# Gate product of the turned weight pieces two slots later, in a fused linear attention and two-MoE kernel on one Trainium2 core

## The chip, the cores and the metric

The kernel runs on 1 core of one Trainium2 chip. The metric is the device time of one execution in microseconds (us), the median of the runs shown.

## The reference

Three layers follow one another, all in float32. Layer 1 is linear attention over 2 batches, 8 heads, 576 positions and head dimension 64, with 128 random features. Its output is laid out as 1152 tokens of width 512. Layer 2 is a dense feed-forward layer over all tokens. Layer 3 sends each token to the one of 8 experts with the largest gate logit, with a capacity of 288 tokens per expert; positions are counted in token order.

```python
q_p, k_p = phi(q * scale), phi(k * scale)          # exp of projections less their maximum
attn = (q_p @ (k_p.T @ v)) / (q_p @ k_p.sum() + 1e-6)
x = attn as [1152, 512]
h = x @ w_in; g = h * (1 / (1 + exp(-1.702 * h)))   # [1152, 2048]
x = g @ w_out                                      # [1152, 512]
logits = x @ w_gate; expert = argmax(logits)       # 8 experts
# each expert takes its first 288 tokens: relu(x @ w1[e]) @ w2[e], scaled by the softmax weight
```

## The kernel before, in words

**Precision.** A float32 matrix product is done as three products on TensorE, of a rounded high part and the remainder (`mm3`, L81 to L84: high by high, high by low, low by high). So every weight and every activation is split into `hi` and `lo`. A split takes a cast on ScalarE and a subtraction on VectorE or GpSimd.

**Tokens and slots.** The 1152 tokens are four groups G of 288. The second layer is cut into 16 slices m of 128 hidden features. A slot n of the list `seq` (L570 to L574) makes one slice of one group: `do_h` (12 matmuls into one of two PSUM banks, then gelu on ScalarE). Two slots later `do_consume` uses the gelu. Groups 0, 1 and 3 are mixed in slots 0 to 47 (the 16 slots of group 2 follow as 48 to 63). From slot 7 to slot 39 the pattern is G = 0, 1, 3, repeated.

For groups 0 and 2 the gelu is split: ScalarE writes `ghi` (L596) and the full value g32 (L598; the trace calls it g), VectorE writes `glo` (L599), and `do_y` multiplies both into the output. For groups 1 and 3 only the routing logits are wanted at first. ScalarE writes one full value g1 (L591), which waits in a list until four of them are there (two of each group). Then `run_lg` (L635 to L641) multiplies them with `wp`, the product of w_out and w_gate for that slice. By the order of the list `run_lg` runs in slots 10, 14, 20, 26, 32, 38, 43, 47 and 49, after the `do_h` of that slot. The values g1 and g32 share the buffers of one tag, `g1`, with five of them; a slot's gelu gets whichever buffer is free.

**Decoding weights.** The weights arrive as 8-byte numbers in 512 KB pieces (two pieces for each slice, one of w_in, one of w_out). `decode` turns a piece into float32 by three VectorE operations (L220, L223, L226), a cast on ScalarE (L232) and a subtraction on GpSimd (L233). Six pieces are decoded during the attention, the other 26 beside the slots by `decode_slot(n)` (L901), one for each slot from slot 9 on (slot 25 has the last). `paced` puts each VectorE step behind the newest `glo` in VectorE's order.

**The gate product.** For `wp` a decoded w_out piece is turned in 32x32 blocks on VectorE (`do_wt`, L481, tile `wt`, one buffer for two slices). For every second slice `do_wg` (L483) multiplies `wt` on TensorE (32 small matmuls, L488), ScalarE copies the result, and one slot later `do_wp` (L494) makes `wp` from it. `do_wg` runs `P["wgl"]` = 2 slots after the decode of the odd slice. The pieces of slices 9, 11, 13 and 15 are decoded in slots 13, 17, 21 and 25, so their gate products stand in slots 15, 19, 23 and 27, at the end of the slot.

**Third layer.** The experts' first products (`do_h2`, 16 slots) use the same tags `ghi` and `glo` for their relu (`hhi`, L832, `hlo`, L833) and the same two PSUM banks. Expert weights are split by ScalarE (L818) and VectorE (L819) beside them.

**Order.** The order in each engine's queue comes from a scheduler that works through the instructions by priority, that is by the order of the program, and takes a buffer for a tile when one is free. Each engine then works its queue in order.

Of the kernel before, what the change touches and what calls it, by code (L numbers as in the profile page):

```python
# [8 lines left out]
F32 = mybir.dt.float32  # L9
F32R = mybir.dt.float32r  # L10
BF16 = mybir.dt.bfloat16
I32 = mybir.dt.int32
ACTF = mybir.ActivationFunctionType
ALU = mybir.AluOpType
AX = mybir.AxisListType.X
P = dict(ahead=2, kvlag=2, t2=3, n=5, x=6, dec=(13, 16, 19, 22, 25, 28), tailstep=0.5, zero=26, w0=12, loadlag=10, pv=(0, 4), l1=3, l3=5, wgl=2, hpt=30, dmin=0.9, dc=1, dd=2, dlead=6, dpace=1)


@with_exitstack
def linear_attention__moe__top1_moe_kernel(  # L20
# [18 lines left out]
    E = moe2_w1.shape[0]  # L39
# [5 lines left out]
    GS = 288  # L45
# [12 lines left out]
    const = ctx.enter_context(tc.tile_pool(name="const", bufs=1, side="left"))  # L58
    xp = ctx.enter_context(tc.tile_pool(name="xp", bufs=1, side="left"))
    gp = ctx.enter_context(tc.tile_pool(name="gp", bufs=3, side="left"))  # L60
# [5 lines left out]
    attB = stB.enter_context(tc.tile_pool(name="attB", bufs=1, side="left", reuse_waits="tile"))  # L66
    stA = ExitStack()
    attA = stA.enter_context(tc.tile_pool(name="attA", bufs=1, side="right", reuse_waits="tile"))
    def bank(tag, name):
        return psA.tile([128, 512], F32, tag=tag, name=name, bufs={"A": 2, "B": 3, "C": 1, "M": 1, "L": 1}[tag])  # L70
# [20 lines left out]
    def load_rows(src, kind, b, p, parts=1):  # L91
        t = attA.tile([128, NU, D], F32, tag="raw", name="qk_raw", bufs=6)
        heads = src[b, 4 * p:4 * p + 4]
        per = 4 // parts
        for i in range(parts):
            hs_ = slice(i * per, (i + 1) * per)
            nc.sync.dma_start(
                out=t[:, JF * per * i:JF * per * (i + 1)].rearrange("p (h j) d -> p h (j d)", j=JF),
                in_=heads[hs_, 0:SF].rearrange("h (p j) d -> p h (j d)", j=JF),
            )  # L100
        for h in range(2):
            nc.sync.dma_start(
                out=t[64 * h:64 * h + 64, 16:18],
                in_=heads.rearrange("(u h) s d -> h s u d", h=2)[h, SF:S],
            )
        raws[kind, b, p] = t
# [93 lines left out]
    def w_in(m):  # L200
        hi, lo = W["in", m // 4]
        c = slice((m % 4) * 128, (m % 4) * 128 + 128)
        return hi[:, :, c], lo[:, :, c]
# [50 lines left out]
    def at(s, f):  # L254
        pend.setdefault(s, []).append(f)
# [70 lines left out]
    def do_kv_out(b, p):  # L326
        t = attB.tile([128, 4, VW], F32, tag="kvs", name="kvs", bufs=4)
        nc.scalar.copy(t.rearrange("p h n -> p (h n)"), kvp.pop((b, p))[:, :4 * VW])
        kvs[b, p] = t
# [71 lines left out]

    npre = len(P["dec"])
    wseq = [(kd, m) for m in range(NF) for kd in ("in", "out")]
# [19 lines left out]
    for kd, b, p in pairs:  # L423
        ps_ = pos[kd, b, p]
        for x in (kd, "v") if kd == "k" else (kd,):
            if (x, b, p) not in raws:
                at(max(0, ps_[0] - P["loadlag"]), lambda x=x, b=b, p=p: load_rows(srcs[x], x, b, p))
        if kd == "k":
            if b > 0:
                at(pos["k", 0, p][4] + P["kvlag"] + 1, lambda b=b, p=p: place_v(b, p))  # L430
            else:
                at(P["pv"][p], lambda p=p: place_v(0, p, mark["M", P["pv"][p]]))
            for d in range(5):
                at(ps_[d] + P["kvlag"], lambda s=ps_[d]: do_KV(s))
            at(ps_[4] + P["kvlag"], lambda b=b, p=p: do_kv_out(b, p))
        else:
# [16 lines left out]
    NB = DM // 32  # L453
# [22 lines left out]
    wts, wus = {}, {}  # L476

    def do_wt(m):
        if m % 2 == 0:
            wts[m // 2] = gp.tile([128, NB, 2, 32], F32, tag="wt", name="wt", bufs=1)  # L480
        nc.vector.transpose(wts[m // 2][:, :, m % 2], wfs.pop(m).rearrange("p (b j) -> p b j", j=32))  # L481

    def do_wg(m):  # L483
# [26 lines left out]
    for s in range(NS + 1):  # L510
# [14 lines left out]
        if s in DEC_AT:  # L525
# [4 lines left out]
            kd, m = wseq[wl[1] - 1]  # L530
# [20 lines left out]


    def const_iota(name, parts, shape, pattern, base, mult):
        ti = const.tile([parts] + shape, I32, name=name + "_i")
        nc.gpsimd.iota(ti, pattern=pattern, base=base, channel_multiplier=mult)
        tf = const.tile([parts] + shape, F32, name=name)
        nc.vector.tensor_copy(tf, ti)
        return tf
# [23 lines left out]
    def do_h(G, m, full=False):  # L582
        tk = slice(G * GS, G * GS + GS)
        hi, lo = w_in(m)
        ps = bank("A", "h_ps")
        for c in range(KD):
            mm3(ps[:, :GS], hi[:, c], lo[:, c], x_hi[:, c, tk], x_lo[:, c, tk],
                c == 0, c == KD - 1)
        if G % 2 and not full:
            g1 = gp.tile([128, GS], F32, tag="g1", name="g1", bufs=5)  # L590
            mark["a"] = nc.scalar.activation(g1, ps[:, :GS], ACTF.Gelu_apprx_sigmoid)  # L591
            gs[G, m] = g1
            return
        ghi = gp.tile([128, GS], F32R, tag="ghi", name="ghi")
        glo = gp.tile([128, GS], F32R, tag="glo", name="glo")
        nc.scalar.activation(ghi, ps[:, :GS], ACTF.Gelu_apprx_sigmoid)  # L596
        g32 = gp.tile([128, GS], F32, tag="g1", name="g32", bufs=5)
        mark["a"] = nc.scalar.activation(g32, ps[:, :GS], ACTF.Gelu_apprx_sigmoid)  # L598
        mark["v"] = nc.vector.tensor_tensor(glo, g32, ghi.bitcast(F32), ALU.subtract)  # L599
        gs[G, m] = (ghi, glo)  # L600
# [19 lines left out]
    def do_lg(G, m):  # L620


        i = G - 1 + m % 2
        if i in lgq:
            run_lg()
        lgq[i] = (m, gs.pop((G, m)))
        if len(lgq) == 4 or (G, m) == (3, NF - 1):
            run_lg()
        if (G, m) == (3, NF - 1):
            held_t.append(gp.tile([128, GS], F32, tag="g1", name="lgt", bufs=5))  # L630
            nc.scalar.copy(held_t[0], held.pop()[:, :GS])

    lgq, held_t = {}, []
# [50 lines left out]
    def do_logits(G):  # L684
        if G % 2 == 0:
            ps = mbank("lg_ps")
            for c in range(KD):
                tk = slice(G * GS, G * GS + GS)
                nc.tensor.matmul(ps[:2 * E, :GS], wg[:, c].rearrange("p a e -> p (a e)"), x_hi[:, c, tk],
                                 start=(c == 0), stop=False)  # L690
                nc.tensor.matmul(ps[:E, :GS], wg[:, c, 0], x_lo[:, c, tk],
                                 start=False, stop=(c == KD - 1))
            t = gp.tile([2 * E, GS], F32, tag="g1", name="lgy", bufs=5)
            nc.scalar.copy(t, ps[:2 * E, :GS])
            n = 2 * E
        else:
            n = 64 if G == 1 else 128
            t = held_t[0]
        ps = mbank("lgr_ps")
        for j in range(TJ):  # L700
            nc.tensor.transpose(
                ps[:TT, j * n:(j + 1) * n], t[:n, j * TT:(j + 1) * TT], ident[:n, :n]
            )
        sl = slice(G * TJ, (G + 1) * TJ)
        a0 = 2 * (G == 3)
        parts = ps[:TT, :TJ * n].rearrange("p (j a e) -> p j e a", j=TJ, e=32 if G % 2 else E)
        nc.vector.tensor_reduce(lg[:, sl], parts[:, :, 0:E, a0:a0 + 2], AX, ALU.add)
        nc.vector.tensor_reduce(mx[:, sl], lg[:, sl], AX, ALU.max)
        cand = small([TT, TJ, E], F32, f"cand{G}")
        first = small([TT, TJ], F32, f"first{G}")  # L710
        bc = [TT, TJ, E]
        nc.vector.tensor_tensor(cand, lg[:, sl], mx[:, sl].unsqueeze(2).to_broadcast(bc), ALU.is_ge)
        nc.vector.tensor_tensor(cand, cand, e_desc.unsqueeze(1).to_broadcast(bc), ALU.mult)
        nc.vector.tensor_reduce(first, cand, AX, ALU.max)
        nc.vector.tensor_tensor(oh[:, sl], cand, first.unsqueeze(2).to_broadcast(bc), ALU.is_equal)
# [107 lines left out]
    def do_h2(key, m, wt, tok):  # L823
        ps = bank("A", "h_ps")
        hi, lo = wt[m // 4]
        fc = slice((m % 4) * 128, (m % 4) * 128 + 128)
        for c in range(KD):
            mm3(ps[:, :GS], hi[:, c, fc], lo[:, c, fc], x_hi[:, c, tok], x_lo[:, c, tok],
                c == 0, c == KD - 1)
        hhi = gp.tile([128, GS], F32R, tag="ghi", name="hhi")  # L830
        hlo = gp.tile([128, GS], F32R, tag="glo", name="hlo")
        nc.scalar.activation(hhi, ps[:, :GS], ACTF.Relu)  # L832
        nc.vector.scalar_tensor_tensor(hlo, ps[:, :GS], 0.0, hhi.bitcast(F32), ALU.max, ALU.subtract)  # L833
        hs[key, m] = (hhi, hlo)
# [80 lines left out]
    for i, (kd, m) in enumerate(wseq[npre:]):  # L915
        need = at_slot[0, m] + (0 if kd == "in" else 2) - P["dlead"]
        n = max(int(i * P["dmin"]), min(need, int(i * P["dpace"])))
# [48 lines left out]
    for n in range(NSL + 2 * NF2 + 2):  # L966
        if n < NSL:
            do_h(*seq[n])
        elif n < NSL + 2 * NF2:
            i, m = divmod(n - NSL, NF2)  # L970
# [5 lines left out]
        elif n >= NSL + 2:  # L976
            i, m = divmod(n - 2 - NSL, NF2)
# [13 lines left out]
    with tc.If(n_left > 0):  # L991
# [23 lines left out]
        with tc.For_i(0, n_left):  # L1015
# [15 lines left out]
            wt = weight_tiles(("in", 2), ("out", 0), ("out", 1), ("out", 2))  # L1031
# [47 lines left out]
```

## Time and profile before

| what | value |
| --- | --- |
| median of the runs | 352.25 us (350.18 to 354.01) |
| the profiled execution | 351.04 us, span of its instructions 349.3 us |
| TensorE (PE) busy | 321.5 us, 92% |
| VectorE (DVE) busy | 211.7 us, 61% |
| ScalarE (ACT) busy | 162.2 us, 46% |
| GpSimd (POOL) busy | 57.5 us, 16% |
| mean granted TensorE clock | 0.977 of full |

PEld is TensorE's weight load, which overlaps its matmuls. PEclk is the granted clock as a share of full speed (1.00 is 2.4 GHz, 0.50 is 1.2 GHz). In a timeline row the first number is the start, the second the duration, and a bracket at the end gives the idle time before it and what ended it. L82, L83 and L84 are the three lines of `mm3`, so their tile names tell which product it is (h_ps: `do_h` or `do_h2`; y: `do_y` or `do_y2`).

### The profile page before, as it was taken

To read this page: it belongs to the slowest core of one execution; us is meant where nothing else is said; L and a number is where in the kernel's file an instruction comes from. 1 tells how busy PE (TensorE), PEld (TensorE's weight loads), DVE (VectorE), ACT (ScalarE), POOL (GpSimd) and SP (SyncE) were. 2 spreads that over 40 slices of the span, in tenths; PEclk is the share of its full clock that TensorE was granted. 3 is DMA by queue.
4 is the path that set the end of the run, shared out by engine and by line. 5 is a ranking of instruction groups with operands and counts; after the bars stand their busy time and mean duration, and the time that the engine had idled before them with its cause. 6 is when DMAs were issued, how large, how long until landed. Compare 5 with 4: busy or idle time off the path is not lost.

```text
span 349.3 us, 7032 instructions
## 1 busy us (share of the span) xinstructions
PE 321.5 (92%) x2745; PEld 303.1 (87%) x2745; DVE 211.7 (61%) x455; ACT 162.2 (46%) x421; POOL 57.5 (16%) x69
## 2 busy tenths in 40 slices
PE   5899998899899999788988999999999999998990
PEld 5899897788898998777877998989999999998990
DVE  6578797897589999999992002316544132567322
ACT  3698887887853434243332224234344233165312
POOL 4111111120032544353541000000000001010000
PEclk9999999999999999898998999999999999999996
DMA  5996832211014455543610000151420000283202
GB/s 164 304 303 158 267 108 87 63 62 61 2 41 143 129 177 179 148 150 128 200 42 2 0 2 0 57 185 27 120 98 1 2 0 2 93 276 114 69 0 77
DMA packets 31192, 35.27 MB, mean 101 GB/s; under 512 B 7472, under 2 KB 25904, under 8 KB 31152
## 3 DMA queue, kind: packets, MB, share of 16 engines
q1 hardware_dynamic: 31152, 34.76, 32.6%
q8 instruction: 23, 0.38, 0.4%
q14 instruction: 17, 0.14, 0.1%
HBM read 32.39 MB, written 2.36 MB: 99 GB/s over the span
## 4 chain that ended last, share of the span: by engine, by line
PE 59%; DVE 25%; ACT 4%; DMA 4%; issue 3%; SPq 2%; DVEq 0%; ACTq 0%
PE h_ps L82 8%; PE h_ps L83 8%; PE h_ps L84 8%; DVE wraw L226 7%; DVE wf L223 6%; PE y L82 5%; PE y L83 5%; PE y L84 5%; DVE wf L220 5%; PE nps L348 4%; PE kvp L323 4%; DMA eraw<-in_moe_w_dram 3%; DVE wt L481 2%; PE t L337 2%; DVE x_lo L383 2%
## 5 line engine op out<-in xcount | busy, mean ns | idle before, releaser
L599 DVE TENSOR_TENSOR glo<-g,ghi 128x288 fp32r<-128x288 f32 x32 | 14.8, 462 | 52.8 <-ACT g L598 52.8
L596 ACT ACTIVATE ghi<-h_ps 128x288 fp32r<-128x288 f32 x32 | 13.1, 411 | 45.2 <-PE h_ps L84 45.2
L591 ACT ACTIVATE g<-h_ps 128x288 f32<-128x288 f32 x32 | 13.2, 412 | 43.6 <-PE h_ps L84 33.0
L226 DVE SCALAR_TENSOR_TENSOR wraw<-wraw,wf 128x512 int32<-128x512 int32 x32 | 31.7, 990 | 2.3
L223 DVE SCALAR_TENSOR_TENSOR wf<-wraw,wf 128x512 int32<-128x512 int32 x32 | 26.6, 832 | 0.8
L292 DVE TENSOR_REDUCE nb<-pj 128x4 f32<-128x512 f32 (+1 forms) x40 | 25.0, 628 | 3.4 <-PE pj L84 3.3
L819 DVE TENSOR_TENSOR el<-eraw,eh 128x1024 fp32r<-128x1024 f32 x16 | 19.5, 1222 | 12.4 <-ACT eh L818 12.4
L82 PE MATMUL pj<-om_hi,xh 128*128 128x256 f32 x72 | 24.1, 334 | 1.6 <-ACT qp L305 1.5
L818 ACT CAST eh<-eraw 128x1024 fp32r<-128x1024 f32 x16 | 16.7, 1048 | 14.1 <-issue 8.3
L220 DVE TENSOR_SCALAR wf<-wraw 128x512 int32<-128x512 int32 x32 | 22.2, 693 | 0.7 <-DMA wraw<-in_moe_w_in_dram 0.4
L889 POOL MEMSET base<- 96x1536 f32 x2 | 2.8, 1380 | 119.1 <-PE h_ps L84 119.1
L305 ACT ACTIVATE qp<-pj,nb 128x128 f32<-128x128 f32 x72 | 21.7, 396 | 0.2 <-DVE nb L292 0.2
L83 PE MATMUL pj<-om_lo,xh 128*128 128x256 f32 x72 | 21.5, 299 | 0.0
L305 ACT ACTIVATE kp<-pj,nb 128x128 f32<-128x128 f32 x72 | 21.3, 383 | 0.0
L84 PE MATMUL pj<-om_hi,xl 128*128 128x256 f32 x72 | 20.9, 290 | 0.0
L323 PE MATMUL kvp<-vt,kp 128*128 128x65 f32 (+1 forms) x144 | 20.6, 269 | 0.1
L82 PE MATMUL h_ps<-x_hi,win1h 128*128 128x288 f32 x64 | 20.5, 320 | 0.0
L82 PE MATMUL h_ps<-x_hi,win2h 128*128 128x288 f32 x64 | 20.4, 318 | 0.0
L82 PE MATMUL h_ps<-x_hi,win0h 128*128 128x288 f32 x64 | 20.0, 312 | 0.0
L82 PE MATMUL y<-hhi,eh 128*128 128x288 f32 x64 | 19.1, 298 | 0.9 <-DVE z L850 0.9
L323 PEld LDWEIGHTS kvp<-vt,kp 128*128 128x128 f32 x144 | 19.0, 191 | 0.8 <-issue 0.3
L83 PE MATMUL h_ps<-x_lo,win2h 128*128 128x288 f32 x64 | 19.7, 308 | 0.0
(210 smaller groups left out, 1081.4 us busy)
## 6 DMA issues: line engine op xcount, KB each, us to landing
wraw<-in_moe_w_in_dram SPq DMA_DIRECT2D x16, 512.0 KB, 3.7
wraw<-in_moe_w_out_dram SPq DMA_DIRECT2D x16, 512.0 KB, 3.7
eraw<-in_moe_w_dram SPq DMA_DIRECT2D x16, 512.0 KB, 4.5
qk_raw<-in_v_dram SPq DMA_DIRECT2D x4, 512.0 KB, 5.2
qk_raw<-in_q_dram SPq DMA_DIRECT2D x4, 512.0 KB, 5.5
qk_raw<-in_k_dram SPq DMA_DIRECT2D x3, 512.0 KB, 5.3
out_dram<-zer SPq DMA_DIRECT2D x2, 576.0 KB, 7.2
out_dram<-base SPq DMA_DIRECT2D x6, 192.0 KB, 2.2
```

The costliest lines, as they stand in the source:

```text
L82: nc.tensor.matmul(o, lh, rh, start=start, stop=False)
L83: nc.tensor.matmul(o, lh, rl, start=False, stop=False)
L84: nc.tensor.matmul(o, ll, rh, start=False, stop=stop)
L220: nc.vector.tensor_scalar(f, high, 3, 0x3FFFFFF8, ALU.logical_shift_left, ALU.bitwise_and)
L223: nc.vector.scalar_tensor_tensor(f, high, -0x40000000, f, ALU.bitwise_and, ALU.bitwise_or)
L226: nc.vector.scalar_tensor_tensor(low, low, 29, f, ALU.logical_shift_right, ALU.bitwise_or)
L292: mark["M", s] = nc.vector.tensor_reduce(nb[:, :nj], pj[:, :nj * M].rearrange("p (a m) -> p a m", m=M), AX, ALU.min)
L305: nc.scalar.activation(t[:, i], pj[:, i * M:(i + 1) * M], ACTF.Exp, bias=nb[:, i:i + 1], scale=-1.0)
L323: nc.tensor.matmul(ps[:, o:o + n], kp[:, i], vts[p][:, u, c0:c0 + n], start=(f == 0), stop=(f == NU - 1))
L599: mark["v"] = nc.vector.tensor_tensor(glo, g32, ghi.bitcast(F32), ALU.subtract)
L818: nc.scalar.copy(hi, tv)
L819: nc.vector.tensor_tensor(lo, tv, hi.bitcast(F32), ALU.subtract)
```

## The change

The gate product moves from two slots to four slots after the decode (`wgl`), and with it the making of `wp`, from three to five. The tile `wt` gets two buffers in place of one. The tags `ghi` and `glo` get two buffers in place of the pool's three, in `do_h` and in `do_h2`. The tag `g1` gets four in place of five. The integer helper tiles of four small tables move from the pool `const`, which stays, to `attB`, which is closed later.

```diff
-P = dict(..., l1=3, l3=5, wgl=2, hpt=30, ...)
+P = dict(..., l1=3, l3=5, wgl=4, hpt=30, ...)
...
-            wts[m // 2] = gp.tile([128, NB, 2, 32], F32, tag="wt", name="wt", bufs=1)
+            wts[m // 2] = gp.tile([128, NB, 2, 32], F32, tag="wt", name="wt", bufs=2)
...
-        ti = const.tile([parts] + shape, I32, name=name + "_i")
+        ti = attB.tile([parts] + shape, I32, name=name + "_i")
...
-            g1 = gp.tile([128, GS], F32, tag="g1", name="g1", bufs=5)
+            g1 = gp.tile([128, GS], F32, tag="g1", name="g1", bufs=4)
...
-        ghi = gp.tile([128, GS], F32R, tag="ghi", name="ghi")
-        glo = gp.tile([128, GS], F32R, tag="glo", name="glo")
+        ghi = gp.tile([128, GS], F32R, tag="ghi", name="ghi", bufs=2)
+        glo = gp.tile([128, GS], F32R, tag="glo", name="glo", bufs=2)
...
-        g32 = gp.tile([128, GS], F32, tag="g1", name="g32", bufs=5)
+        g32 = gp.tile([128, GS], F32, tag="g1", name="g32", bufs=4)
...
-        hhi = gp.tile([128, GS], F32R, tag="ghi", name="hhi")
-        hlo = gp.tile([128, GS], F32R, tag="glo", name="hlo")
+        hhi = gp.tile([128, GS], F32R, tag="ghi", name="hhi", bufs=2)
+        hlo = gp.tile([128, GS], F32R, tag="glo", name="hlo", bufs=2)
```

The two further tiles of tag `g1` (L630 and L693) also say four in place of five.

## Rows read from the trace of the kernel before

**Rows 1.** Busy time by stretch: start:end, length, each engine, clock, DMA share, GB/s.

```profile
104.00:142.60 38.60, 38.02 (x398) 34.78 (x396) 36.65 (x55) 15.55 (x37) 15.71 (x11) 1.00 0.52 158
...
185.60:190.00 4.40, 4.40 (x36) 4.10 (x36) 0.46 (x1) 0.99 (x4) 0.50 (x1) 0.61 0.02 4
...
190.00:240.00 50.00, 50.00 (x385) 45.98 (x384) 9.11 (x40) 13.17 (x34) 0.00 (x0) 1.00 0.13 43
```

**Rows 2.** Waits in 142 to 190: waiter, releaser, us in total, times, longest.

```profile
PE wg_ps L488 <- DVE wt L481: 7.8, 4, 2.8
...
ACT g L591 <- DVE glo L599: 3.2, 1, 3.2
```

**Rows 3.** Timeline of PE: the gate products of slots 15, 19 and 23.

```profile
144.92 0.92 PE L488 MATMUL wg_ps<-wt,wgd 128*32 128x64 f32 x32 [2.03 <-DVE wt L481]
...
158.49 0.84 PE L488 MATMUL wg_ps<-wt,wgd 128*32 128x64 f32 x32 [2.80 <-DVE wt L481]
...
170.53 0.65 PE L488 MATMUL wg_ps<-wt,wgd 128*32 128x64 f32 x32 [0.80 <-DVE wt L481]
```

**Rows 4.** Timeline of DVE: two decodes, glo of slots 22 and 25, last wt.

```profile
154.02 0.69 DVE L226 SCALAR_TENSOR_TENSOR wraw<-wraw,wf 128x512 int32<-128x512 int32 x1
...
156.00 1.59 DVE L226 SCALAR_TENSOR_TENSOR wraw<-wraw,wf 128x512 int32<-128x512 int32 x1
...
170.31 0.82 DVE L599 TENSOR_TENSOR glo<-g,ghi 128x288 fp32r<-128x288 f32 x1
...
180.57 0.45 DVE L599 TENSOR_TENSOR glo<-g,ghi 128x288 fp32r<-128x288 f32 x1
...
184.05 0.71 DVE L481 STREAM_TRANSPOSE wt<-wraw 128x512 f32<-128x512 f32 x1
```

**Rows 5.** Timeline of PE, slots 27 to 30, around the last gate product.

```profile
181.08 0.40 PE L83 MATMUL y<-glo,wout2h 128*128 128x288 f32 x1 [0.33 <-DVE glo L599]
...
182.50 0.29 PE L84 MATMUL y<-ghi,wout2l 128*128 128x288 f32 x1
...
184.91 0.65 PE L488 MATMUL wg_ps<-wt,wgd 128*32 128x64 f32 x32 [2.12 <-DVE wt L481]
...
186.13 0.44 PE L83 MATMUL h_ps<-x_lo,win3h 128*128 128x288 f32 x1
...
192.27 0.30 PE L82 MATMUL y<-ghi,wout3h 128*128 128x288 f32 x1
```

**Rows 6.** Timeline of PE: the run of slot 43 and the next slice.

```profile
222.79 0.67 PE L640 MATMUL lgt_ps<-g,wp 128*8 128x288 f32 x8
...
223.40 0.40 PE L82 MATMUL h_ps<-x_hi,win3h 128*128 128x288 f32 x1
```

**Rows 7.** Timeline of ACT: gelu of slots 42 and 43.

```profile
221.18 0.41 ACT L591 ACTIVATE g<-h_ps 128x288 f32<-128x288 f32 x1 [1.25 <-PE pos_ps L728]
...
223.48 0.41 ACT L591 ACTIVATE g<-h_ps 128x288 f32<-128x288 f32 x1 [1.89 <-PE lgt_ps L640]
```

**Rows 8.** Timeline of ACT, tail of the attention: gelu of slot 2 and an attention cast.

```profile
99.26 0.41 ACT L596 ACTIVATE ghi<-h_ps 128x288 fp32r<-128x288 f32 x1 [0.24 <-PE h_ps L84]
...
102.05 1.11 ACT L382 CAST x_hi<-xps 128x512 fp32r<-128x512 f32 x1 [0.65 <-PE xps L390]
```

**Rows 9.** Timelines of PE and DVE there: end of y of slot 2, attention's x_lo.

```profile
102.39 0.30 PE L84 MATMUL y<-ghi,wout0l 128*128 128x288 f32 x1
...
103.20 1.09 DVE L383 TENSOR_TENSOR x_lo<-xps,x_hi 128x512 fp32r<-128x512 f32 x1 [0.35 <-ACT x_hi L382]
```

**Rows 10.** Timeline of ACT beside the first expert: relu, and a split after its load.

```profile
306.48 0.41 ACT L832 ACTIVATE hhi<-h_ps 128x288 fp32r<-128x288 f32 x1
...
310.06 1.05 ACT L818 CAST eh<-eraw 128x1024 fp32r<-128x1024 f32 x1 [2.16 <-DMA eraw<-in_moe_w_dram]
```

**Rows 11.** Timeline of PE there: last matmul of y in that slot.

```profile
307.75 0.29 PE L84 MATMUL y<-hhi,el 128*128 128x288 f32 x1
```

**Rows 12.** Timeline of POOL: one subtraction of a weight piece.

```profile
155.50 1.55 POOL L233 TENSOR_TENSOR win2l<-wraw,win2h 128x512 fp32r<-128x512 f32 x1 [2.13 <-ACT win2h L232]
```

More of the change, by code (lines that the diff above doesn't have):

```diff
@@ L15 @@
 AX = mybir.AxisListType.X
-P = dict(ahead=2, kvlag=2, t2=3, n=5, x=6, dec=(13, 16, 19, 22, 25, 28), tailstep=0.5, zero=26, w0=12, loadlag=10, pv=(0, 4), l1=3, l3=5, wgl=2, hpt=30, dmin=0.9, dc=1, dd=2, dlead=6, dpace=1)
+P = dict(ahead=2, kvlag=2, t2=3, n=5, x=6, dec=(13, 16, 19, 22, 25, 28), tailstep=0.5, zero=26, w0=12, loadlag=10, pv=(0, 4), l1=3, l3=5, wgl=4, hpt=30, dmin=0.9, dc=1, dd=2, dlead=6, dpace=1)
 @with_exitstack
@@ L629, in do_lg @@
         if (G, m) == (3, NF - 1):
-            held_t.append(gp.tile([128, GS], F32, tag="g1", name="lgt", bufs=5))
+            held_t.append(gp.tile([128, GS], F32, tag="g1", name="lgt", bufs=4))
             nc.scalar.copy(held_t[0], held.pop()[:, :GS])
@@ L692, in do_logits @@
                                  start=False, stop=(c == KD - 1))
-            t = gp.tile([2 * E, GS], F32, tag="g1", name="lgy", bufs=5)
+            t = gp.tile([2 * E, GS], F32, tag="g1", name="lgy", bufs=4)
             nc.scalar.copy(t, ps[:2 * E, :GS])
```

## The prediction, made before the changed kernel was run

> **What bounds the kernel now.** I read the busy time by stretch first. From 104 to 142.6 us both PE and VectorE are full; from 190 on PE is full (50.00 of 50.00) and VectorE nearly idle [rows 1]. Between them lies the only stretch where PE, the bound of the rest, stands still. The table of waits says on what: 7.8 us in four waits of the gate product for the turned piece `wt` [rows 2]. Three are in slots 15, 19 and 23, of 2.03, 2.80 and 0.80 us [rows 3], the fourth in slot 27, of 2.12 us [rows 5].
>
> VectorE's timeline shows why. It decodes without a pause, some 3 us a piece, and is late: the last `wt` ends at 184.05 + 0.71 = 184.76 [rows 4], and the gate product starts at 184.91 [rows 5]. After that wait the granted clock falls: mean 0.61 from 185.6 to 190, matmuls of 0.44 us where 0.29 is usual [rows 1, 5].
>
> **Why the four waits are not the gain.** `do_y` of slot 27 also waits for VectorE: its second matmul starts at 181.08, just behind `glo` of slot 25, which ends at 180.57 + 0.45 = 181.02 [rows 4, 5]. That `glo` stands behind the decodes of all earlier slots in VectorE's queue, and VectorE does not idle. So whatever PE saves in slots 15 to 23, it stands at y of slot 27 until 181.08 again; the waits there change their name, from `wt` to `glo`. The gate product now has four slots from decode to use; y has only two from `glo`, and becomes the next late thing. What counts is what PE does after 181.08.
>
> **The parts.**
>
> 1. *Gate product of slot 27 goes to slot 29.* Matmuls follow one another by 50.00/385 = 0.13 us [rows 1], so behind y of slot 27 PE could go on at 182.50 + 0.13 = 182.63; it stands to 184.91, 2.28 us [rows 5]. In slot 29 it comes behind two products of 12 matmuls, 12 × 0.13 = 1.56 us each, so not before 185.75; `wt` has been there since 184.76. The wait goes. With it goes the slow stretch behind it, 4.40 × (1 − 0.61) = 1.72 us [rows 1]. The work itself (0.59 us, 184.91 to 185.50) is done before y of slot 30 in both. Y of slot 30 needs `glo` of slot 28, right behind the last `wt` in VectorE's queue. Slot 28's product ends near 184.3, two gelus of 0.41 [rows 7] and a `glo` of 0.45 take 1.3 us, and PE needs 3.7 (two products and the gate product) to arrive: covered. Gain 4.0 us. Its bounds are 2.28 (the clock falls anyway, because PE stood ahead of y) and 4.0.
>
>    Will it fall? From y of slot 24 (`glo` ready at 170.31 + 0.82 = 171.13) to y of slot 27 lie 9.9 us, and PE has 4 products of 1.6, a gate product of 0.6, a run of 0.6 and the stop of part 2 of 0.55: 8.15 us. It stands 1.7 us at most, less if it was slow before. The wait of 0.80 was followed by usual matmuls, that of 2.12 by slow ones [rows 3, 5]. I take "stays full", being only a little over half likely.
>
> 2. *Four buffers of tag g1, not five.* This is the part that costs. At `run_lg` of slots 14, 20, 26, 32, 38, 43 and 47 four values wait in the list, and g32 or g1 of the slot before needs a fifth buffer. That five are just enough now can be seen: the gelu of slot 43, a sixth, waits for the run and starts at 223.48, while that of slot 42 ran at 221.18, free [rows 7]; and the gelu of slot 26 waits 3.2 us for a `glo` to free its buffer [rows 2]. With four, the gelu of the slot before the run starts behind the run. It holds one of the two PSUM banks, the product of that slot's `do_h`; the other bank is held by the slot of the run. So the next `do_h` can't start behind the run, as it does at 223.40 [rows 6], but only behind the gelu, at 223.48 + 0.41 + about 0.06 (the step from `glo` to y above) = 223.95: 0.55 us each. In slots 14, 20 and 26 PE would have stood at y in any case: nothing. In 32, 38, 43 and 47 PE is the bound: 4 × 0.55 = 2.2 us lost. Bounds: 0 (the scheduler fills the gap) and 7 × 0.55 = 3.9.
>
>    Would VectorE idle, since `glo` of slots 13, 19 and 25 comes later? The run of slot 26 ends at 171.13 + 3 × 1.6 + 0.6 + 0.6, some 177.1 (178.9 behind a slow stretch); a gelu later is still ahead of 180.57, when VectorE takes that of slot 25 [rows 4]. I take the other two alike, PE being ahead of VectorE there too. Nothing; an idle VectorE would be priced as in D.
>
> 3. *Two buffers of ghi and glo.* While groups are mixed y frees one in time. Where every slot writes one (group 2, the experts), `ghi` of slot n must wait for y of slot n − 2, which stands on PE right behind slot n's `do_h`: a shift of 1.6 us out of 3.2 a slot, and y of slot n comes 4.8 us after. The bank is free in time too. Beside the first expert the relu at 306.48 would wait for the end of y, 307.75 + 0.29, some 1.6 us, and a split behind it too; the split after that waits for its load until 310.06 anyway [rows 10, 11]. 0 to 0.5 us; I take 0.2.
>
> 4. *Second wt buffer, helper tiles:* no instruction is added, no transfer moved; and no turn waits for a gate product now (the table of waits has none), so the second buffer only keeps that so. 0. SyncE's loads wait for GpSimd's subtractions, and these for the cast behind a gelu; part 2 puts them later in slots 13, 19 and 25. A piece is loaded four decodes, some 12 us, ahead: 0, with D as the price if not.
>
> Sum: −4.0 + 2.2 + 0.2 = −1.6 us. Against the profiled execution: 351.04 − 1.6 = 349.4. That one stands 1.2 below the median of the runs, 352.25; so **350.7 us**, 0.5% less than before.
>
> **Rivals.**
>
> *A. The runs' stops are hidden* (the scheduler puts the run ahead, or gives the gelu a buffer): only −4.0 + 0.2, 348.4 us. For it: the order is not written out by hand. Against it: the four values are alive until the run, and the last one is the gelu of two slots before. 15%.
>
> *B. The wait takes another place and the clock falls there:* PE stands ahead of y of slot 27 and runs slow after 181 instead of after 185. −2.3 + 2.2 + 0.2 = +0.1, 352.3 us. For it: 1.7 us lies nearer to 2.03 and 2.12, after which the clock fell, than to 0.80. 22%.
>
> *C. Slower: ScalarE stops at the tail of the attention.* Slots 0 to 3 are all of group 0, so with two buffers `ghi` of slot 2, at 99.26, must wait for the end of y of slot 2, 102.39 + 0.30 = 102.69: 3.4 us [rows 8, 9]. If it keeps its place in ScalarE's queue, the attention's cast at 102.05 comes 2.8 us later (between the two ScalarE works 2.14 us and idles 0.65: 102.69 + 2.14 = 104.83), VectorE's x_lo at 103.20 behind it as much, and the whole row of decodes, which has no slack, ends 2.8 later. −1.6 + 2.8 = +1.2: 353.5 us; with the price of B, 355.2. It turns slower from 1.6 us of delay at 103.20 on, that is 2.25 at 99.26, as the 0.65 are slack. Against it: a tile without a free buffer is not queued, and the casts behind it are ready. 12%.
>
> *D. The decodes take another time.* The same L226 takes 0.69 us alone and 1.59 beside GpSimd's subtraction of 155.50 [rows 4, 12]. Part 2 shifts casts, and so subtractions, in slots 13, 19 and 25. If three of them hit an operation more, or one less, VectorE's row is 3 × 0.9 = 2.7 us longer or shorter: 353.4 or 348.0 us, counted from 350.7. A shift alone trades one hit for another, hence 8%. The Trainium skill (SBUF — State Buffer, Who interferes with whom) says that a VectorE instruction with two SBUF inputs and a GpSimd one that reads SBUF exclude each other for a whole instruction; the rows agree: the 1.59 end 0.54 us after GpSimd's 1.55. By that rule a subtraction that meets a turn of one input (0.71 at 184.05, [rows 4]) would cost VectorE nothing, which would make the shorter half of D, 348.0 us, the likelier one; no row here shows a turn so met, and I leave the halves even.
>
> **The numbers.** My forecast has 43%: 350.7. Over 1%, or 3.5 us, is about what a measurement of this kernel tells from no change. Faster by that (348.7 or less): A and half of D, 0.18 with some of A lost to spread. Slower by that (355.8 or more): part of C with B's price, and the runs' own spread, 0.08. Within 1%: 0.74. The range takes in A at the bottom and C and D at the top: 348.2 to 353.5.
>
> **What would show it.** The waits of the gate product for `wt` are gone; `do_y` in slots 18, 21 and 24 waits 1 to 3 us for `glo`, and that of slot 27 starts again near 181; the last `wt` still ends near 184.8. From 182.6 on the clock is full (B: 0.6 for some 4 us). After the runs of slots 32, 38, 43 and 47 the next `do_h` starts 0.55 us later than the end of the run (A: at once), and the gelu before the run names the run as its releaser. `ghi` of group 2 waits for y. I am wrong if VectorE's last `wt` moves by more than 1 us (C, D), or if PE idles by more than 1 us in the expert's stretch.

## The result, and the profile after

The changed kernel takes 352.88 us in the median of 20 runs, the kernel before 350.17 in as many (the 352.25 shown ahead of the prediction was the median of its first three). The ratio is 1.0073, 95% interval 1.0052 to 1.0093: 0.7% or some 2.6 us **slower**, where the forecast was 0.5% or 1.6 us faster. The time lies in the range forecast, and the change is less than 1%; the sign is wrong, by 4.2 us.

The profiled execution took 352.35 us, its span is 350.5. First the head of the page of the changed kernel: engine, busy time, share of the span, instructions.

```profile
PE 319.9 (91%) x2745; PEld 301.2 (86%) x2745; DVE 215.0 (61%) x455; ACT 161.8 (46%) x421; POOL 58.0 (17%) x69
```

PE is busy for 1.6 us less than before, VectorE for 3.3 us more. The waits from 142 to 195 us (waiter, releaser, sum, times, longest) answer to [rows 2]:

```profile
PE y L83 <- DVE glo L599: 6.3, 4, 2.2
ACT g L598 <- PE lgt_ps L640: 6.0, 3, 2.1
```

No wait of the gate product is left; in its place y waits for `glo`, and there is one wait that the kernel before doesn't have at all, of the full gelu (L598) for a run. PE's timeline of the changed kernel (start, duration, and in brackets the idle time before it) answers to [rows 3] and [rows 5]:

```profile
153.46 0.40 PE L83 MATMUL y<-glo,wout2h 128*128 128x288 f32 x1 [1.74 <-DVE glo L599]
...
166.25 0.65 PE L488 MATMUL wg_ps<-wt,wgd 128*32 128x64 f32 x32
...
174.66 0.61 PE L83 MATMUL y<-glo,wout2h 128*128 128x288 f32 x1 [2.21 <-DVE glo L599]
...
185.19 0.40 PE L83 MATMUL y<-glo,wout2h 128*128 128x288 f32 x1 [0.53 <-DVE glo L599]
...
189.90 0.65 PE L488 MATMUL wg_ps<-wt,wgd 128*32 128x64 f32 x32
```

Y of slot 27 starts again at 185.19, not near 181: 4.11 us later than before. VectorE shows why: its last `wt`, at 184.05 before [rows 4], comes at 188.14.

```profile
188.14 0.71 DVE L481 STREAM_TRANSPOSE wt<-wraw 128x512 f32<-128x512 f32 x1
```

From there on PE makes good what the forecast said: the run of slot 32 starts at 197.50, 0.34 us later than before (197.16), so 3.8 of the 4.1 us are back. Then it loses again: the run of slot 49 starts at 235.56 (before 233.98), 1.58 late. PE's last transposes, at the end of the experts' stretch, start at 342.68 (before 341.23), 1.45 late. So there are three amounts to explain: the late decodes, 4.1 us, the gain, 3.8, and a loss of 1.2 between the runs of slots 32 and 49. (These two profiled executions, 351.04 and 352.35, are only 1.3 us apart; the medians differ by more.)

**The late decodes begin at the tail of the attention.** The fifth `wt` (slice 4) starts at 113.19 for 110.63, already 2.56 us late. ScalarE, VectorE and GpSimd of the changed kernel there:

```profile
102.05 1.08 ACT L382 CAST x_hi<-xps 128x512 fp32r<-128x512 f32 x1 [2.09 <-PE xps L390]
102.92 0.45 ACT L596 ACTIVATE ghi<-h_ps 128x288 fp32r<-128x288 f32 x1
...
103.55 0.64 ACT L232 CAST win0h<-wraw 128x512 fp32r<-128x512 f32 x1
...
103.16 1.08 DVE L383 TENSOR_TENSOR x_lo<-xps,x_hi 128x512 fp32r<-128x512 f32 x1 [1.16 <-ACT x_hi L382]
104.15 0.41 DVE L368 TENSOR_TENSOR xr<-nps,den 128x256 f32<-128x256 f32 x1
104.48 1.37 DVE L220 TENSOR_SCALAR wf<-wraw 128x512 int32<-128x512 int32 x1
105.78 1.57 DVE L599 TENSOR_TENSOR glo<-g,ghi 128x288 fp32r<-128x288 f32 x1
...
104.27 1.30 POOL L233 TENSOR_TENSOR win0l<-wraw,win0h 128x512 fp32r<-128x512 f32 x1 [25.99 <-ACT win0h L232]
105.53 1.50 POOL L233 TENSOR_TENSOR wout0l<-wraw,wout0h 128x512 fp32r<-128x512 f32 x1
```

And the kernel before: the decode's cast, a turn, the decode's L220, `glo` and GpSimd's two subtractions:

```profile
100.17 0.67 ACT L232 CAST win0h<-wraw 128x512 fp32r<-128x512 f32 x1
...
101.25 0.70 DVE L481 STREAM_TRANSPOSE wt<-wraw 128x512 f32<-128x512 f32 x1
...
101.93 0.59 DVE L220 TENSOR_SCALAR wf<-wraw 128x512 int32<-128x512 int32 x1
...
104.81 0.45 DVE L599 TENSOR_TENSOR glo<-g,ghi 128x288 fp32r<-128x288 f32 x1
...
100.92 1.31 POOL L233 TENSOR_TENSOR win0l<-wraw,win0h 128x512 fp32r<-128x512 f32 x1 [22.64 <-ACT win0h L232]
102.20 1.50 POOL L233 TENSOR_TENSOR wout0l<-wraw,wout0h 128x512 fp32r<-128x512 f32 x1
```

With two buffers `ghi` of slot 2 comes at 102.92, not at 99.26 [rows 8]. The attention's cast does not stand behind it and keeps its 102.05. But the decode's two casts do: the program itself queues each of them behind the newest gelu (`paced` at L909 works on ScalarE's order as it does on VectorE's). So they and GpSimd's two subtractions behind them move by 3.4 us with `ghi`, the subtractions from beside a turn and a partly idle VectorE to beside L220 and `glo`, which take 1.37 for 0.59 and 1.57 for 0.45: 1.90 us. And L220 now stands behind the first `x_lo`, so VectorE idles for 1.16 us ahead of that where it idled 0.35 [rows 9]: 0.81. Together 2.71, and the next `x_lo` starts at 109.04 for 106.32. PE pays behind that: it stands 2.33 us for VectorE (`xm`) at 110.75, where it stood 0.46 before.

### The profile page after: what moved, and what is told of

It is laid out like the page before. It is cut to its first block, busy times and chain, and to the rows that moved or that the text cites. A ratio compares the mean times of both kernels' runs of the same rounds, so it can differ in the third digit from the quotient of the medians.

```text
span 350.5 us, 7052 instructions
## 1 busy us (share of the span) xinstructions
PE 319.9 (91%) x2745; PEld 301.2 (86%) x2745; DVE 215.0 (61%) x455; ACT 161.8 (46%) x421; POOL 58.0 (17%) x69
## 4 chain that ended last, share of the span: by engine, by line
PE 60%; DVE 23%; issue 4%; ACT 4%; DMA 4%; SPq 2%; DVEq 0%; ACTq 0%
PE h_ps L82 8%; PE h_ps L83 8%; PE h_ps L84 8%; DVE wraw L226 6%; DVE wf L223 6%; PE y L83 5%; PE y L82 5%; PE y L84 5%; PE nps L348 4%; DVE wf L220 4%; PE kvp L323 4%; PE t L337 2%; ACT x_hi L382 2%; DMA eraw<-in_moe_w_dram 2%; DVE wt L481 2%
## 5 line engine op out<-in xcount | busy, mean ns | idle before, releaser
L599 DVE TENSOR_TENSOR glo<-g,ghi 128x288 fp32r<-128x288 f32 x32 | 18.4, 574 | 51.2 <-ACT g L598 51.0
L223 DVE SCALAR_TENSOR_TENSOR wf<-wraw,wf 128x512 int32<-128x512 int32 x32 | 28.7, 897 | 0.8
L220 DVE TENSOR_SCALAR wf<-wraw 128x512 int32<-128x512 int32 x32 | 19.7, 617 | 1.5 <-DMA wraw<-in_moe_w_in_dram 1.2
L82 PE MATMUL h_ps<-x_hi,eh 128*128 128x288 f32 x64 | 19.3, 302 | 1.4 <-DVE hlo L833 1.4
L82 PE MATMUL h_ps<-x_hi,win1h 128*128 128x288 f32 x64 | 19.7, 307 | 0.0
L833 DVE SCALAR_TENSOR_TENSOR hlo<-h_ps,hhi 128x288 fp32r<-128x288 f32 x16 | 7.3, 455 | 20.1 <-ACT hhi L832 19.9
L82 PE MATMUL h_ps<-x_hi,win3h 128*128 128x288 f32 x64 | 19.2, 300 | 0.5 <-ACT g L591 0.5
L82 PE MATMUL h_ps<-x_hi,win2h 128*128 128x288 f32 x64 | 19.6, 306 | 0.0
```

The lines of the kernel that those rows point to most:

```text
L82: nc.tensor.matmul(o, lh, rh, start=start, stop=False)
L220: nc.vector.tensor_scalar(f, high, 3, 0x3FFFFFF8, ALU.logical_shift_left, ALU.bitwise_and)
L223: nc.vector.scalar_tensor_tensor(f, high, -0x40000000, f, ALU.bitwise_and, ALU.bitwise_or)
```

## The experiments

Theory: the move is good, and what pays for its second `wt` buffer, one buffer less of `ghi`, `glo` and `g1` each, costs more. Rivals: the move itself makes the decodes late; or only collisions with GpSimd do. The ratios below are all to the kernel before, with 95% intervals; 0.001 is 0.35 us, and the differences in us are worked out from the ratios. The runs are called e1 to h4.

**The three parts, each alone.** E1 is the kernel before with the move alone:

```diff
-P = dict(..., wgl=2, ...)
+P = dict(..., wgl=4, ...)
```

> The kernel before with the gate product alone moved (wgl=4; one wt buffer, five g1, three ghi and glo as before). Theory 1 (the move is good and the smaller buffers lose more than it gains): no wait of the gate product for wt, the last wt still near 184.8 us, 3.5 to 4.2 us less than before, ratio 0.988 to 0.990. Rival R (the move itself makes VectorE's decodes late, by another order of its instructions): last wt 2 to 4 us later, ratio 0.998 to 1.008. Rival W (with one wt buffer the turn of the next pair stands behind the gate product): VectorE waits for PE wg, last wt 1 to 3 us later, ratio 0.993 to 1.000.

Measured: 345.49 us, ratio **0.9858** (0.9828 to 0.9888), 5.0 us less. Theory 1, and somewhat more than it: last `wt` at 183.61, the gate product waits nowhere, and no wait of VectorE for it shows, with one `wt` buffer. Y of slot 27 doesn't wait for `glo` either. VectorE's `glo` of slot 25 comes ahead of the turn:

```profile
179.75 0.45 DVE L599 TENSOR_TENSOR glo<-g,ghi 128x288 fp32r<-128x288 f32 x1
180.12 0.70 DVE L481 STREAM_TRANSPOSE wt<-wraw 128x512 f32<-128x512 f32 x1
```

and PE is full, with the clock at 1.00, in the window from 180 to 190 (columns as in [rows 1]):

```profile
180.00:190.00 10.00, 10.00 (x116) 9.56 (x115) 5.21 (x7) 3.83 (x11) 3.00 (x2) 1.00 0.01 2
```

E2 is the kernel before with two buffers of `ghi` and `glo` (in all four tiles of these tags), still with `wgl=2`:

```diff
-        ghi = gp.tile([128, GS], F32R, tag="ghi", name="ghi")
+        ghi = gp.tile([128, GS], F32R, tag="ghi", name="ghi", bufs=2)
...
```

> The kernel before with two buffers of ghi and glo alone. Theory 1: ghi of slot 2 waits for y of slot 2's elder, the casts and VectorE's x_lo at the tail of the attention come some 3 us later, so does the whole row of decodes (last wt near 187.5 us instead of 184.8), and PE's y of slot 27 with it: 2.5 to 3.5 us more than before, ratio 1.007 to 1.010. Rival R (the buffers are harmless): ratio 0.999 to 1.002, last wt within 0.5 us of before.

Measured: 353.91 us, ratio **1.0112** (1.0075 to 1.0149), 3.9 us more. Fifth `wt` at 113.58 (2.95 later); the last one at 190.91, 6.9 later, in the profiled execution, which was the slowest of this kernel's runs (356.69). So two buffers are not harmless, and they cost more than Theory 1 has. The delay is larger than the tail's here in part because VectorE idled for another 2.37 us for a gelu at 121.39. Ahead of that PE had stood 2.32 us for VectorE at 110.91, and the granted clock was 0.50 from 112 to 118.

E3 is the kernel before with four buffers of `g1` (in all four tiles):

```diff
-            g1 = gp.tile([128, GS], F32, tag="g1", name="g1", bufs=5)
+            g1 = gp.tile([128, GS], F32, tag="g1", name="g1", bufs=4)
...
```

> The kernel before with four buffers of tag g1 alone. Theory 1: PE stands for 0.5 us behind the runs of slots 43 and 47 and the scheduler fills the gap behind those of 32 and 38: 1.0 us more, ratio 1.002 to 1.004. The forecast's own price: 2.2 us, ratio 1.006. Rival D (the later casts make GpSimd's subtractions meet more of VectorE's operations): the glo of L599 grow by 2 us or more in sum and the last wt comes 1 to 2 us later, ratio 1.005 to 1.010.

Measured: 354.89 us, ratio **1.0131** (1.0094 to 1.0167), 4.6 us more: twice the forecast's price. None of the three named its cause. The fifth `wt` is near its old place (111.10), but between two later ones (157.45 and 166.99) the row falls back by 3.7 us. PE, ScalarE and VectorE there:

```profile
161.03 1.15 PE L640 MATMUL lgt_ps<-g,wp 128*8 128x288 f32 x8
...
162.19 0.41 ACT L598 ACTIVATE g<-h_ps 128x288 f32<-128x288 f32 x1 [2.97 <-PE lgt_ps L640]
...
162.64 0.46 DVE L599 TENSOR_TENSOR glo<-g,ghi 128x288 fp32r<-128x288 f32 x1 [2.65 <-ACT g L598]
```

This is to be read from below: VectorE idles for 2.65 us, because its next instruction is the `glo` of slot 19; that needs the full gelu, which waits for a buffer until the run of slot 20 has ended, at 161.03 + 1.15 = 162.18. The same happens at 184.51 (1.60) for slot 25. VectorE is the engine that this stretch depends on, so its idle time goes into the total.

**Slot 2's buffers given back.** In e4, the changed kernel otherwise, `ghi` and `glo` of slot 2 alone take buffers of the tag `g1`, which is idle at that time (`glo` by the same edit):

```diff
-        ghi = gp.tile([128, GS], F32R, tag="ghi", name="ghi", bufs=2)
+        ghi = gp.tile([128, GS], F32R, tag="ghi" if seq.index((G, m)) != 2 else "g1", name="ghi", bufs=2 if seq.index((G, m)) != 2 else 4)
...
```

> The changed kernel, but ghi and glo of slot 2 take buffers of the tag g1, which nothing else uses at that time, so that the tail of the attention doesn't wait. Theory 1: ghi of slot 2 near 99.3 us again, wt of slice 4 near 110.6 instead of 113.2, last wt 2.6 us earlier than 188.1, 2.6 us less than the changed kernel, ratio to the kernel before 0.999 to 1.001. Rival (the decodes are late for another cause that comes later, such as the collisions with GpSimd): last wt within 1 us of 188.1, ratio 1.005 to 1.008.

Measured: 349.37 us, ratio **0.9980** (0.9960 to 1.0000): 3.3 us less than the changed kernel. `ghi` at 99.40, fifth `wt` at 110.66, last one at 184.85, so 2.53 of the 3.29 us were lost by slice 4 and 0.76 behind it. That is Theory 1, and a little more than it: the buffers of one slot. The 18.4 us that the `glo` of the changed kernel take in sum (14.8 before) fall with it:

```profile
L599 DVE TENSOR_TENSOR glo<-g,ghi 128x288 fp32r<-128x288 f32 x32 | 15.5, 486 | 53.5 <-ACT g L598 53.5
```

**The prices beside the move.** F1 is e1 with the edit of e2, f2 is e1 with the edit of e3. F3 is the changed kernel with one buffer of `wt` (and the helper tiles back in `const`):

```diff
-            wts[m // 2] = gp.tile([128, NB, 2, 32], F32, tag="wt", name="wt", bufs=2)
+            wts[m // 2] = gp.tile([128, NB, 2, 32], F32, tag="wt", name="wt", bufs=1)
```

> The gate product moved and two buffers of ghi and glo; five g1, one wt buffer. Theory 1 (two ghi cost the decodes some 2.6 us at the tail of the attention, and PE follows them): wt of slice 4 and last wt some 2.6 us later than with the gate product alone moved (last wt near 186.2), 2.6 us more than that, ratio to the kernel before 0.992 to 0.995. Rival (the price of 3.9 us that two ghi had alone stays whole, since its larger part is an idle VectorE and a slow clock, not the tail): ratio 0.996 to 0.999.

> The gate product moved and four buffers of g1; three ghi and glo, one wt buffer. Theory 1 (with the gate product out of the way the runs come early enough, VectorE does not idle for g32, and only the stops behind the runs of slots 43 and 47 are left, 1.2 us): ratio 0.989 to 0.991, last wt within 0.7 us of 183.6. Rival (four g1 cost the same 4.6 us as alone, VectorE idles 2 us or more for the gelu of slots 19 and 25): ratio 0.997 to 1.000.

> The changed kernel with one buffer of wt in place of two (the helper tiles where they were): PE, ScalarE, GpSimd and the queues have the same order, VectorE's turns stand later in its order. Theory 1 (the second buffer is worth nothing): the changed kernel's time, ratio 1.006 to 1.009. Theory 2 (turns that stand later let glo of slot 25 go first, which PE's y of slot 27 waits for): 1 to 2 us less, 1.001 to 1.005. Theory 3 (turns then wait for PE): 1.010 or more, last wt after 189.

Measured: f1 348.92 us, **0.9981** (0.9961 to 1.0000), 4.3 us above e1. That is the rival's number; by the profile the last `wt` is at 185.23, 1.6 later than e1's, but the execution profiled (348.52) and e1's (346.44) lie on opposite sides of their medians. So the loss at slot 2 is confirmed. What makes more of it than 2.6 shows in part. Where `ghi` of slot 2 is late (the changed kernel, e2, f1, f3) PE stands 2.32 to 2.35 us for VectorE near 110.8; in all other runs it stands 0.44 to 0.49 us at that place. Behind that the clock fell to 0.50 in the profiled executions of e2, f1 and f3, for 3 to 7 us, and in that of the changed kernel it stayed at 1.00. The changed kernel, and below it f1:

```profile
110.75 0.63 PE L398 MATMUL xps<-fold,xm 128*128 128x64 f32 x4 [2.33 <-DVE xm L378]
```

```profile
110.56 0.99 PE L398 MATMUL xps<-fold,xm 128*128 128x64 f32 x4 [2.32 <-DVE xm L378]
...
116.11 0.71 DVE L481 STREAM_TRANSPOSE wt<-wraw 128x512 f32<-128x512 f32 x1 [1.15 <-PE wg_ps L488]
```

With the slow PE VectorE then stands for PE: 2.37 us in e2, 1.15 in f1 (the last row: the turn waits for a gate product), 2.48 in f3, in the changed kernel not at all. That the clock is what brings these stops is argued from one execution of each; the kernels differ too.

f2 350.05 us, **1.0004** (0.9984 to 1.0025), 5.1 us above e1: the rival's number, not its place. VectorE does not idle for the gelus of slots 19 and 25, but at 131.13 (0.68) and 140.71 (0.73) for gelus behind earlier runs (e1: once, 0.91); `glo` of slot 25 ends at 181.76 (e1: 180.20), and y of slot 27 waits again, 1.67 us. So four buffers don't become cheap with the gate product out of the way.

f3 353.66 us, **1.0096** (1.0069 to 1.0123), against 1.0073 of the changed kernel: by the ratios the second `wt` buffer is worth 0.8 us, and the intervals overlap. Only VectorE's order differs in it; with one buffer its turns stand later, and it idles for 2.48 us at 117.73 for a gate product, and 0.68 and 0.72 at 135.71 and 145.28 for gelus; the last `wt` comes at 189.72. By the trace that is Theory 3, but the slow clock (0.50 from 111 to 117) is in its longest stop; by the time it can't be told from Theory 1. Theory 2 is out.

**The price of four g1, split.** In h1, e4 otherwise, the gelus of four slots in which a run stands take the decoder's buffer `wf`, idle from slot 27 on:

```diff
-            g1 = gp.tile([128, GS], F32, tag="g1", name="g1", bufs=4)
+            g1 = gp.tile([128, GS], F32, tag="g1", name="g1", bufs=4) if seq.index((G, m)) not in (32, 38, 43, 47) else gp.tile([128, DM], I32, tag="wf", name="g1", bufs=1)[:, :GS].bitcast(F32)
```

In h2, f2 otherwise, the full gelus of slots 13, 19 and 25 take the third `ghi` buffer, idle there:

```diff
-        g32 = gp.tile([128, GS], F32, tag="g1", name="g32", bufs=4)
+        g32 = gp.tile([128, GS], F32, tag="g1", name="g32", bufs=4) if seq.index((G, m)) not in (13, 19, 25) else gp.tile([128, GS], F32R, tag="ghi", name="g32").bitcast(F32)
```

> The changed kernel with ghi and glo of slot 2 in buffers of g1 (as in e4) and, besides, the gelus of slots 32, 38, 43 and 47 in the decoder's buffer wf, which is idle from slot 27 on: behind the runs it is as with five g1. Theory 1 (the late part of the price of four g1 is the two stops behind the runs of slots 43 and 47): both waits gone, 1.2 us less than e4, ratio to the kernel before 0.993 to 0.996. Rival (the stops are hidden by what follows): e4's time, 0.997 to 1.000.

> The gate product moved and four buffers of g1 (as in f2), but the full gelus of slots 13, 19 and 25 in a buffer of the tag ghi, of which one is idle there: VectorE has the order of instructions that it has with five g1. Theory 1 (the early part of the price is that these gelus stand behind the runs, glo behind them, and PE's y behind glo): no gelu of slots 13, 19 and 25 waits for a run, no idle VectorE, y of slot 27 doesn't wait, only the two late stops of 0.5 us are left: 1.2 us more than with the gate product alone moved, ratio 0.988 to 0.991. Rival (the stops behind the late runs are the whole price): f2's time, ratio 0.999 to 1.002.

Measured: h1 347.75 us, **0.9944** (0.9918 to 0.9971), 1.3 us below e4. h2 346.93 us, **0.9906** (0.9890 to 0.9923), 3.4 us below f2. Both as Theory 1 has it. In h1 both stops are gone. In the changed kernel PE's timeline shows them, and ScalarE's their reason, two gelus held by one run:

```profile
223.21 0.67 PE L640 MATMUL lgt_ps<-g,wp 128*8 128x288 f32 x8
224.37 0.40 PE L82 MATMUL h_ps<-x_hi,win3h 128*128 128x288 f32 x1 [0.48 <-ACT g L591]
...
230.96 0.67 PE L640 MATMUL lgt_ps<-g,wp 128*8 128x288 f32 x8
232.17 0.40 PE L82 MATMUL h_ps<-x_hi,win0h 128*128 128x288 f32 x1 [0.54 <-ACT g L591]
```

```profile
223.90 0.71 ACT L591 ACTIVATE g<-h_ps 128x288 f32<-128x288 f32 x2 [3.50 <-PE lgt_ps L640]
```

In [rows 6, 7] the next product started right behind the run, and only one gelu waited. In h2 VectorE has the same order as in e1 and no gelu of slots 13, 19 and 25 waits for a run. Y of slot 27 waits 0.23 us, in f2 1.67, and the run of slot 32 starts at 193.06, in e1 at 193.09. From there to the run of slot 49 h2 needs 38.04 us, e1 36.81: the two late stops. They are worth 1.2 to 1.3 us, the early half is worth 3.4 by the ratios. Only 1.1 us of that can be placed: in f2's profiled execution the run of slot 32 starts at 194.14.

**Where else do two ghi cost?** H3 and h4 are f1 (the move, two buffers of `ghi` and `glo`) with those of slot 2 in `g1`, of which h3 has five buffers and h4 seven; `glo` by the same edit:

```diff
-        ghi = gp.tile([128, GS], F32R, tag="ghi", name="ghi", bufs=2)
+        ghi = gp.tile([128, GS], F32R, tag="ghi" if seq.index((G, m)) != 2 else "g1", name="ghi", bufs=2 if seq.index((G, m)) != 2 else 5)
...
```

> The gate product moved, two buffers of ghi and glo, and those of slot 2 in buffers of g1; five g1, one wt buffer. Theory 1 (slot 2 is the only place where two ghi cost anything): the time with the gate product alone moved, ratio 0.984 to 0.989, wt of slice 4 near 113.1 us and the last wt near 183.6. Rival (slot 3, group 2 or the experts' relus pay for the second buffer too): 0.990 to 0.996.

> As h3_g5_slot2_own with seven buffers of g1 for five. The order of all engines is the same as with five. Theory 1 (five are just enough): the same time, ratio 0.984 to 0.989. Rival (the gelus of slots 20 and 26, which wait up to 3.3 us for a glo to free their buffer, hold PE's bank): those waits gone and 1 to 2 us less, ratio 0.979 to 0.984.

Measured: h3 346.73 us, **0.9898** (0.9882 to 0.9915); h4 346.74, **0.9916** (0.9894 to 0.9938). The two don't differ, so five buffers of `g1` are just enough and more are worth nothing. Against e1 h3 is 1.4 us longer, with intervals that just overlap: of the 4.3 us of f1 some 2.9 are slot 2's, and whether the rest of the kernel pays the other 1.4 stays open. The profile has no place for it: the stretch from the run of slot 32 to the last transposes is 143.76 us (191.19 to 334.95) and 143.71 in e1 (193.09 to 336.80), and h3's profiled execution is the shorter of the two (344.36, e1's 346.44).

**Is one slot enough?** F4 is the kernel before with `wgl=3`:

```diff
-P = dict(..., wgl=2, ...)
+P = dict(..., wgl=3, ...)
```

> The kernel before with the gate product one slot later instead of two (wgl=3), all buffers as before. A slot is some 2.4 us of PE beside a VectorE that needs 3 us a piece, and the four waits were 0.8 to 2.8 us: theory 1: the waits for wt vanish too, ratio 0.986 to 0.990, like wgl=4. Rival: the waits of slots 15 and 19 stay in part (0.5 us or more) and with them a slow clock, ratio 0.990 to 0.997.

Measured: 348.48 us in the median of eleven runs (ten from 347.50 to 349.39, one of 1051.34), **0.9950** (0.9934 to 0.9966): the rival. The gate product still waits for 0.52, 1.72 and 0.51 us.

```profile
160.08 0.65 PE L488 MATMUL wg_ps<-wt,wgd 128*32 128x64 f32 x32 [1.72 <-DVE wt L481]
...
173.78 0.40 PE L83 MATMUL y<-glo,wout2h 128*128 128x288 f32 x1 [3.51 <-DVE glo L599]
```

Two slots are needed (no run has more), and e1, one number changed in the kernel before, is the version that beats both: 1.4% less than before, 2.1% less than the changed kernel (0.9858/1.0073 = 0.979).

## Why the prediction was wrong

**The sum.** The forecast was −4.0 + 2.2 + 0.2. The runs give −5.0 (e1), +5.1 (four g1, f2 less e1) and +4.3 (two ghi, f1 less e1), in sum +4.4; each of the two differences is known to about 1.3 us. F3, with all three, has +3.4. That the two losses overlap, since both make the same row late, would fit, but the 1.0 us between is within the noise. So is the 0.8 that the second `wt` takes off; +2.6 are left.

**Step 1, the gate product: right.** It is 5.0 us, 4.0 being within its interval (−6.0 to −3.9). In the changed kernel 3.8 come behind y of slot 27, and the renamed waits in slots 18 to 27 are as forecast (1.74, 1.79, 2.21 and 0.53 us). "It stands at y of slot 27 until 181.08 again" held for the changed kernel in kind, 4.1 us later. In e1 PE doesn't stand there, since VectorE takes `glo` of slot 25 ahead of the turn; but the same matmul starts at 180.74, so even there only 0.34 us are gained ahead of it and 3.73 between it and the run of slot 32. The clock, which rival B has falling from y of slot 27 on, stayed full there (columns as in [rows 1]):

```profile
170.00:180.00 10.00, 7.79 (x75) 7.30 (x74) 9.41 (x13) 3.01 (x7) 3.99 (x3) 0.83 0.56 163
180.00:190.00 10.00, 9.47 (x92) 8.50 (x96) 8.99 (x11) 3.89 (x10) 4.50 (x4) 1.00 0.01 2
```

It fell earlier (0.83 from 150 to 160 as well), where VectorE sets the pace: to 0.50 behind the waits of 1.74 and 2.21 us, and not behind that of 1.79. In e1 it fell behind one of 2.03 us at 171.11 and not behind one of 2.25 at 161.21. So the length of the wait, from which the prediction judged, doesn't order them, and that it stayed full behind y of slot 27 was in part luck.

**Step 3, two buffers of ghi and glo: this one failed, at 0.2 for 4.3 us.** "While groups are mixed y frees one in time" holds from slot 4 on; slots 0 to 3 are all of group 0, which the prediction knew and gave to rival C with 12%. C named the place (slot 2 at 99.26), the row that has no slack, and a size of 2.8 us (2.56 measured at slice 4). Its condition, that `ghi` keeps its place in ScalarE's queue, did not hold. The argument against it ("a tile without a free buffer is not queued, and the casts behind it are ready") came true for the attention's cast and not for the decode's two, which L909 ties to the newest gelu. It was taken as an acquittal, and was none: the delayed gelu took the decode's casts, two subtractions of GpSimd and VectorE's order with it. So C's loss came at C's place, and 1.90 of its 2.71 us by the mechanism of D; the prediction had the two apart, at 12% and 8%, and never as one. By the runs slot 2 is 2.9 of the 4.3 us (f1 less h3), and where the other 1.4 lie stays open.

**Step 2, four buffers of g1: half right, at 2.2 for 5.1 us.** Of "4 × 0.55 = 2.2" two stops came, 0.48 and 0.54 us; without them the kernel is 1.3 us shorter (h1). Behind the runs of slots 32 and 38 the gelu waits, 1.77 us, but the scheduler put four matmuls of y into the gap, as rival A has it. What failed is "In slots 14, 20 and 26 PE would have stood at y in any case: nothing" with "I take the other two alike": that looked at PE and at one of three places on VectorE. The gelus of slots 13, 19 and 25 stand behind the runs and `glo` behind them: 3.4 us (h2). In e3 `glo` is VectorE's next instruction, and VectorE idles for it. In f2 the gelu of slot 25 comes at 177.83, well ahead of 180.57 as the prediction has it [rows 4], but its `glo` takes a later place in VectorE's order, 181.35 for 179.75 in e1. In the changed kernel the run of slot 26, forecast to end near 177.1, starts at 181.65 and that gelu comes at 182.34; slot 2's delay is in that, for in e4 it comes at 177.94.

**Step 4: right as far as it was seen.** Nothing waits for loads, and the second `wt` buffer is worth 0.8 us, not clear of nothing. The end is right, too: from the run of slot 49 to the last transposes the changed kernel takes 107.12 us, before 107.25, so by these two profiles neither group 2 nor the experts pay for two buffers. PE's wait of 1.43 us for an `hlo` at 313.98 stands for the two of 0.56 and 0.37 us for `z` that were there.

**D.** From "no row here shows a turn so met" the prediction left the halves of D even. The rows are there (the turn at 101.25 of the kernel before, above, took its 0.70 inside a subtraction), and they go by the rule (below), but the rule did not make the shorter half likelier: the moved subtractions met L220 and `glo`, not turns.

## What to carry to other kernels

A buffer that is taken away is priced at the first place where it is missing, and on the engine that sets the pace there, not only on the one whose stop is easy to see: here it was ScalarE that lost a buffer and VectorE that paid. If a scheduler reorders around a missing buffer, ask what moves with the delayed instruction and whom that meets. And where a change brings its own payment (here a second buffer and the memory for it), cost the change without the payment first: a move by two slots alone gained 1.4%.

## What the runs showed of the hardware

VectorE's operations meet GpSimd's subtraction unequally. At the tail of the attention L220, with one input in SBUF, took 1.37 us beside a subtraction and 0.59 in the kernel before, and the 128x512 turn never grew: over the traces of all 14 kernels here 67 turns overlapped a subtraction by more than 0.3 us, and they took 0.69 to 0.71 us; the other 157 took 0.68 to 0.74. The turns are one line of this table of the changed kernel (sum and mean in ns behind the bar), L220 another:

```profile
L223 DVE SCALAR_TENSOR_TENSOR wf<-wraw,wf 128x512 int32<-128x512 int32 x32 | 28.7, 897 | 0.8
L220 DVE TENSOR_SCALAR wf<-wraw 128x512 int32<-128x512 int32 x32 | 19.7, 617 | 1.5 <-DMA wraw<-in_moe_w_in_dram 1.2
L481 DVE STREAM_TRANSPOSE wt<-wraw 128x512 f32<-128x512 f32 x16 | 11.3, 709 | 0.7
```

The Trainium skill (SBUF — State Buffer, Who interferes with whom) says that a one-input operation contends with GpSimd only in a two-port mode, and lists the tensor-scalar operation among those that can enter one. The traces agree: L220, a tensor-scalar operation, takes 0.38 to 0.43 us undisturbed and up to 1.55 beside a subtraction, and the turn isn't lengthened. Which mode an instruction ran in no trace here shows.
